# Attention and experts on one core: side work on eight of eighteen steps, a first list over two groups, and a cast of the queries that waits for the lower halves

## The chip, the cores and the metric

The kernel runs on one core of one Trainium2 chip. The metric is the device time of one execution in microseconds (us). The engines are named as in the profile: PE is TensorE (PEld its weight loads), DVE VectorE, ACT ScalarE, POOL GpSimd, SP SyncE, which issues most of the transfers. L12 is line 12 of the kernel before.

## What is computed

An attention whose queries are averaged in pairs, and behind it a mixture of experts with one expert for each token. The reference, cut:

```python
# q, k, v: (8, 8, 1152, 64): batch, heads, sequence, head width
q_pool = q.reshape(B, H, S // 2, 2, D).mean(axis=3)
scores = np.matmul(q_pool, k.transpose(0, 1, 3, 2)) / np.sqrt(D)
attn = np.exp(scores - np.max(scores, axis=-1, keepdims=True))
attn = attn / (np.sum(attn, axis=-1, keepdims=True) + 1e-09)
x = np.matmul(attn, v)               # then (batch, position, head * width): 4608 tokens of 512
# experts: w_gate (512, 8), modality_bias (2, 8), w1 (8, 512, 1024), w2 (8, 1024, 512)
logits = x @ w_gate + modality_bias[modality_id]
e_idx = np.argmax(logits, axis=1)
gate_w = softmax(logits)[token, e_idx]
out[token] = gate_w * (np.maximum(x[token] @ w1[e_idx], 0.0) @ w2[e_idx])
```

The outputs are float32. The kernel reaches this with 16-bit floats: a number is split into a high part and a rest ("hi" and "lo", "qh" and "lo", "VH" and "vl"), and the products of both parts are added up.

## The kernel before

**Attention (0 to about 735 us).** Two batches of one head make a *pair* of heads; there are 32 pairs and 18 *steps* for each, so a pair takes about 22 us. In one step TensorE makes the scores of a third of a row block (L906, L907, tile `psc`), ScalarE their exponentials (L908, tile `Pe`), and VectorE or ScalarE their *lower halves* (the low 16 bits of the exponential, L891 and L889, tile `Pl`); three steps later TensorE multiplies `Pe` and `Pl` with the values (L965 to L967, tile `xp`).

**The max pass.** The scores need the maximum of each query's row before their exponentials. It is found one pair ahead: the max pass of pair p begins 24 steps before the pair's own first step (T_MAX), one matmul of the rounded queries `QB` with the rounded keys `hi` a step (L839, tile `pm`), and a maximum on VectorE (L840). The result `mr` goes by a transfer (L820) into one row of `B`, the matrix that the scores read. There are two `QB`, for even and odd pairs.

**What is prepared for a pair.** The loads of keys and queries (L643, L644) are 46 steps ahead; GpSimd's sum of neighbouring queries (L658, `split_q`) is 34 steps ahead; its cast to 16 bits, `qh` (L667, `split_qh`), 26 steps ahead, and behind it two transfers (L628) put `qh` into `QB`. Then come the rests `lo` (L695, three operations on GpSimd, two of them issued 26 steps ahead), and the transfers of all of it into `B`. The value's high part `VH` is on GpSimd (L786), 14 and 15 steps ahead.

**Holds.** `hold(x, y)` makes the instruction x of GpSimd wait for the instruction y of VectorE, though it needs none of its data. `fast[0]` is the L891 that was issued last, and with `p > HELD` the sum of the queries, one operation of VH and one of lo are held on it, another lo on VectorE's `vl` of the pair before. The cast L667 isn't held.

**Scales.** Each pair's x is scaled by a power of two. `scales` (L753) makes five small operations on VectorE: `half`, two columns of `sc`, a column of `scales` and 64 rows of `both` (L757); one of them holds what another has.

**Side work.** The router's work goes on between the steps: one generator after another in the list `side`, which may make a piece at the end of a step. A group is eight pairs (1152 tokens, nine tiles of 128); there are four. At the end of each group's last pair `route(g)` is put into the list, and behind group 2 `first_list`, which counts the tokens of each expert in the first three groups (27 tiles), gives each token its place in a block (`place`, L459 to L505) and then makes lists of token numbers by small matmuls (`listing`, L507 to L556). It holds its listing until step 576 - 127 (T_LIST). What is left at the end of the attention is made before the experts start.

**The order.** The order of PE, ACT, DVE and POOL is the order of the program; SP's order is made by the framework's scheduler. POOL and SP wait in order: an instruction that waits holds up those behind it.

**Experts (about 735 to 1125 us).** Blocks of 256 tokens of one expert: tokens are gathered from `xs` in HBM by number, multiplied with w1 and w2, and scattered to the output. The first six blocks (NA) take their tokens from the first list. The first block's w1 comes in four loads (L1595) that are issued in the last pair, at steps 1 to 3 of it, into the buffers of the raw queries, keys and values; ScalarE splits them (L1599).

Of the kernel before, what the change touches and what calls it, by code (L numbers as in the profile page):

```python
# [9 lines left out]
F32 = mybir.dt.float32  # L10
# [12 lines left out]
P = 128  # L23
# [5 lines left out]
S = 1152  # L29
# [9 lines left out]
NSTEP = 2 * NKC  # L39
NR = 4  # L40
W3 = 3 * SQ
HELD = 3
BANK = W3 // 4
T_LIST = -127
PL = 2
RS = (4, 4, 2, 2)
SLOW_P = 1
# [71 lines left out]
SW = 3  # L119
PR = 2  # L120
NF = 4
T_W0 = (1, 3, 2, 3)
W1D = 0
T_W1 = (6, 4, 10, 11)
E1 = 1
# [40 lines left out]
class Router:  # L166
# [11 lines left out]
    def setup(self, ids, w_gate, bias):  # L178
        nc, con = self.nc, self.con
        wg = con.tile([P, 4, E], F32, name="wg")  # L180
        nc.sync.dma_start(out=wg, in_=w_gate.rearrange("(c p) e -> p c e", p=P))
        self.wg = con.tile([P, 4, 3, E], BF16, name="wg3")
        for i in range(3):
            nc.gpsimd.tensor_copy(self.wg[:, :, i], wg)
            if i < 2:
                nc.gpsimd.tensor_tensor(wg, wg, self.wg[:, :, i], op=ALU.subtract)
        self.b0 = con.tile([P, 2, E], F32, name="bias")
        nc.sync.dma_start(out=self.b0, in_=bias.rearrange("m e -> (m e)").unsqueeze(0).broadcast_to([P, 2 * E]).rearrange("p (m e) -> p m e", m=2))
        idt = con.tile([P, NTT, 2], I32, name="idt")
        nc.sync.dma_start(out=idt.rearrange("p t w -> p (t w)"), in_=ids.bitcast(I32))  # L190
        self.mid = con.tile([P, NTT], F32, name="mid")
        nc.gpsimd.tensor_copy(self.mid, idt[:, :, 0])
        self.up = con.tile([P, P], BF16, name="up")
        nc.gpsimd.memset(self.up, 1.0)
        nc.gpsimd.affine_select(out=self.up, in_=self.up, pattern=[[1, P]], compare_op=ALU.is_gt, fill=0.0, base=0, channel_multiplier=-1)
        self.id16 = con.tile([P, P], F16, name="id16")
        nc.gpsimd.tensor_copy(self.id16, self.ident)
        self.on = con.tile([P, P], BF16, name="on")
        nc.gpsimd.memset(self.on, 1.0)
        self.ie = self.iota("ie", E)  # L200
        self.ieE = self.iota("ieE", E, base=-E)
        self.lane16 = con.tile([P, P], BF16, name="lane16")
        nc.gpsimd.tensor_copy(self.lane16, self.iota("lane", P))
        self.part = self.iota("part", 1, cm=1)
        self.tile1 = self.iota("tile1", NTT, base=1)
        self.col = self.iota("col", 2 * (NBF - NA) + E)
        self.before = con.tile([P, E + 1, E], F32, name="before")
        nc.gpsimd.memset(self.before, 1.0)
        nc.gpsimd.affine_select(out=self.before, in_=self.before, pattern=[[1, E + 1], [-1, E]], compare_op=ALU.is_gt, fill=0.0, base=0,
                                channel_multiplier=0)  # L210
# [5 lines left out]
        self.added = {g: 0 for g in range(NTT // NT)}  # L216
        z = con.tile([P, NT, 2], F32, name="z")
        nc.gpsimd.memset(z, 0.0)
        nc.sync.dma_start(out=self.xs[T - NT * P:T, DM:XW].rearrange("(t p) d -> p t d", p=P), in_=z)
        self.pos = con.tile([P, NTT], F32, name="pos")  # L220
        self.exp = con.tile([P, NTT], F32, name="exp")

    def iota(self, name, n, base=0, cm=0):
        a = self.sm.tile([P, P], I32, name="io")[:, 0:n]
# [12 lines left out]
        self.nc.scalar.activation(w, self.wg[:, cc], AF.Copy, scale=isc)  # L237
        return w

    def token_scale(self, p, isc):  # L240
# [4 lines left out]
        isc(self.scales[g][:, h:h + 1])  # L245

    def turned(self, x, o):

# [127 lines left out]
    def first_blocks(self):  # L376
# [26 lines left out]
        c3 = sm.tile([P, NA, E], F32, name="own3A")  # L403
        nc.vector.tensor_tensor(c3, self.col[:, 0:NA].unsqueeze(2).broadcast_to([P, NA, E]), cut[:, 1:].unsqueeze(1).broadcast_to([P, NA, E]), op=ALU.is_ge)
        yield
        ef = sm.tile([P, NA], F32, name="ownA")
        nc.vector.tensor_reduce(ef, c3, op=ALU.add, axis=AX.X)
        yield
        self.ownA = self.con.tile([P, NA], I32, name="ownerA")
        nc.vector.tensor_single_scalar(self.ownA, ef, float(E - 1), op=ALU.min)  # L410

    def other_blocks(self):
        nc, sm = self.nc, self.sm
# [43 lines left out]
    def place(self, nt, late):  # L457
# [4 lines left out]
        wide = lambda i: sm.tile([P, nt, E], F32, name=f"ohp{nt}_{i}") if late else sm.tile([P, 3, NT, E], F32, name=f"wide{i}").rearrange("p q t e -> p (q t) e")  # L462
        oh = wide(0)
        nc.vector.tensor_tensor(oh, self.exp[:, 0:nt].unsqueeze(2).broadcast_to([P, nt, E]), be(self.ie), op=ALU.is_equal)
        yield
# [89 lines left out]
    def indices(self, n, acc, name):  # L555
# [10 lines left out]
        nc.vector.scalar_tensor_tensor(si, m, BIG, v, op0=ALU.mult, op1=ALU.add)  # L566
        return gi, si

    def first_list(self):

        for _ in self.first_blocks():
            yield 1
        for _ in self.place(3 * NT, False):
            yield PL
        yield T_LIST
        acc = self.con.tile([P, 2, 2 * NA], F32, name="accA")
        yield from self.listing(3, 2 * NA, acc)
        self.idxA = self.indices(2 * NA, acc, "A")

    def other_list(self):  # L580
# [7 lines left out]
def attention(tc, ctx, att, ident, npairs, xpool, on_two, on_split, on_scale, jobs, side, set_pm, started, ahead, hip):  # L588
# [36 lines left out]
        assert all((p, n) in made for n in names), f"pair {p}: {names} are not made yet"  # L625

    def move(o, i):
        nc.sync.dma_start(out=o, in_=i)  # L628

    half_q = lambda i: slice(i * 288, (i + 1) * 288)  # L630

# [30 lines left out]
    def split_qh(p):  # L662
        s = st[p]
        qh = s["qh"]
        made.add((p, "qh"))
        if p > 1:
            (nc.gpsimd if QH_POOL else nc.vector).tensor_copy(qh, s["q"][:, 0:SQ])  # L667
# [53 lines left out]
    def place_k(p, heads):  # L721

        s = st[p]
        for i in range(2):
            for j in heads:
                move(s["B1"][half[i], kcol(j)], s["hi"][half[j]])

    def place_lo(p, heads, k):

# [22 lines left out]
    def scales(p, pt):  # L752
        s = st[p]  # L753
        half = sm.tile([P, 1], I32, name="half", bufs=1)
        nc.vector.tensor_single_scalar(half, pt[:, 0:1].bitcast(I32), 24, op=ALU.logical_shift_right)
        sc = sm.tile([P, 2], I32, name="sc")
        power_of = lambda o, h, sign, e: nc.vector.tensor_scalar(o, h, sign * 2.0 ** 23, e * 2.0 ** 23, op0=ALU.mult, op1=ALU.add)  # L757
        power_of(sc[:, 0:1], half, -1, 205)
        power_of(sc[:, 1:2], half, 1, 49)
        s["sc"], s["isc"] = sc.bitcast(F32)[:, 0:1], sc.bitcast(F32)[:, 1:2]  # L760
        on_scale(p, lambda o: power_of(o, half, 1, 49))
        if p % 2 == 0:
            s["both"] = xpool.tile([P, 1], I32, name="both", bufs=3)
        r = slice(p % 2 * D, (p % 2 + 1) * D)
        power_of(st[p - p % 2]["both"][r], half[r], 1, 49)

    flat = lambda a: a.rearrange("p c j d -> p (c j) d")

# [149 lines left out]
    def split_x(p, x2):  # L918

        s = st[p]  # L920
        if p % 2 == 0:
            s["x"] = [xpool.tile([P, NT, 2 * D], F16, name=f"x{i}", bufs=1) for i in range(2)]
        hs = slice((p % 2) * D, (p % 2 + 1) * D)
        xh, xl = st[p - p % 2]["x"]
        nc.scalar.activation(xh[:, :, hs], x2[:, :, hs], AF.Copy, scale=s["sc"])
        if p % 2:
            s["xt"] = [xpool.tile([P, NT, P], F16, name=f"xt{i}", bufs=1) for i in range(2)]
            turn_part(p, 0, xh)
        later(XL, lambda: split_xl(p, x2))

    def split_xl(p, x2):
# [4 lines left out]
        if p % 2:  # L936
            turns.append(lambda: turned(p, xh, xl))
            if p + 2 >= npairs or (p + 2, "row9") in made:
                turns.pop(0)()

    def turned(p, xh, xl):
        s = st[p]
# [157 lines left out]
        busy(2)  # L1100
        advance(mxq, 1)
    busy(2)
    at(T_RT, 0, started)

    for p in range(npairs):
        b = NSTEP * p
# [27 lines left out]
    if ahead:  # L1134
        last = (npairs - 1) * NSTEP
        room = []

        def early():
            a, *r = [pa.tile([P, S], F32, name="raw" + x) for x in "qqkkv"]
            room.extend(r)  # L1140
            ahead[0](a)

        at(last + T_G0, 0, early)
        at(last + T_X0, 0, lambda: running.append(ahead[1](lambda: ps_max.tile([P, 512], F32, name="pm"))))
        for i in range(NF):
            at(last + T_W0[i], 0, lambda i=i: ahead[2](i, room[i]))
            at(last + T_W1[i], 0, lambda i=i: later_end(W1D, ahead[3](i)))
    running, wait = [], 0
    for t in range(NSTEP * npairs):
# [20 lines left out]
        if side and t >= wait:  # L1170
            r = next(side[0], DONE)
            if r is DONE:
                side.pop(0)
            else:
                wait = t + (r or 1) if (r or 1) > 0 else NSTEP * npairs + r
    for t in range(NSTEP * npairs, NSTEP * npairs + 40):
        now[0] = t
        advance(pvq, 9)
# [16 lines left out]
def gather_x(nc, rt, j, tile_):  # L1195

    x = []
    for h in parts(j):
        x.append(tile_(h))
        nc.gpsimd.indirect_dma_start(out=x[h][:, :], out_offset=None, in_=rt.xs[0:3 * NT * P if j < NA else T, :],  # L1200
                                     in_offset=bass.IndirectOffsetOnAxis(ap=index(rt, j, h)[0], axis=0))
    return x

# [345 lines left out]
def attention_moe(tc, att, ids, w_gate, bias, w1, w2, out):  # L1549
    nc = tc.nc  # L1550
    with ExitStack() as ctx:
# [9 lines left out]
        def on_two(n, x2):  # L1561
# [96 lines left out]
```

## Time and profile before

| | us |
|---|---|
| median of three runs | 1127.4 (1127.33 to 1129.1) |
| the profiled execution | 1126.72 |
| its span in the profile | 1125.0 |
| of this, TensorE busy | 1102.0 |
| VectorE busy | 972.0 |
| ScalarE busy | 913.3 |
| GpSimd busy | 414.2 |

All of the trace is from the profiled execution; its time has 1.7 us around the span. The clock that TensorE was granted is 1.00 in all stretches shown below. How to read the rows: in the timeline a row is the start and the duration in us, the engine, the line, the operation, the tiles out<-in and the shape, and in brackets how long the engine had been idle and what ended that. In a group by line, "x64 | 6.9, 149" is 64 instructions, 6.9 us busy, 149 ns for one. In the table by stretch a cell is an engine's busy time with its instructions.

### The profile page before, as it was taken

Reading aid. Unit: us, or ns where it says so; the run is one execution under the profiler, and the core shown is the slowest. Engines: PE = TensorE matmul, PEld = TensorE weight load, DVE = VectorE, ACT = ScalarE, POOL = GpSimd, SP = SyncE. Lnnn points to the kernel's source line nnn. Section 1 sums busy time; section 2 is a strip of 40 time slices with the busy share of each in tenths; the row PEclk is TensorE's granted clock in tenths of the full one; section 3 lists DMA queues with packets and bytes.
Section 4 is the critical chain, followed back from the end, with each engine's and each line's share of the span. In section 5 each row is a group of like instructions: output and inputs, shape, how many; then the busy total and the mean of one; then the engine's idle time right before and its main releaser. Section 6 shows DMA issues by size and latency. Waiting matters only on the chain.

```text
span 1125.0 us, 36836 instructions
## 1 busy us (share of the span) xinstructions
PE 1102.0 (98%) x15069; PEld 812.7 (72%) x15069; DVE 972.0 (86%) x1971; ACT 913.3 (81%) x1465; POOL 414.2 (37%) x408
## 2 busy tenths in 40 slices
PE   7999999999999999999999999999999999999997
PEld 3777777777777777777777777777667667667665
DVE  7999999999999999999999999877996766756755
ACT  5999999999999999999999998876556656655654
POOL 7753344355434444443445334115213112122111
PEclk9999999999999999999999999999999999999999
DMA  7777757768669578678687663499999999899993
GB/s 231 181 186 169 197 159 189 188 158 187 171 165 210 152 176 183 165 185 182 171 183 171 160 147 97 144 302 289 285 264 278 299 286 267 279 280 262 296 269 110
DMA packets 175522, 232.67 MB, mean 207 GB/s; under 512 B 92303, under 2 KB 126751, under 8 KB 175344
## 3 DMA queue, kind: packets, MB, share of 16 engines
q1 hardware_dynamic: 169254, 210.45, 71.4%
q0 software_dynamic: 6080, 19.78, 6.7%
q8 instruction: 120, 1.97, 0.8%
q14 instruction: 58, 0.48, 0.1%
q10 hardware_dynamic: 10, 0.00, 0.0%
HBM read 146.11 MB, written 18.99 MB: 147 GB/s over the span
## 4 chain that ended last, share of the span: by engine, by line
PE 80%; DVE 16%; DMA 2%; issue 1%; ACT 1%; SPq 0%; POOL 0%; POOLq 0%; DVEq 0%
PE psc L907 9%; PE psc L906 9%; PE pm L839 8%; DVE mp L840 8%; PE xp L965 6%; PE xp L967 6%; PE ph L1318 6%; PE ph L1316 6%; PE ph L1317 6%; PE xp L966 6%; PE po L1423 6%; PE po L1425 6%; PE po L1424 6%; DVE Pl L891 2%; DVE vl L782 1%; DVE mp L848 1%
## 5 line engine op out<-in xcount | busy, mean ns | idle before, releaser
L908 ACT ACTIVATE Pe<-psc 128x432 int32<-128x432 f32 x768 | 376.8, 526 | 40.6 <-PE psc L907 32.2
L840 DVE TENSOR_REDUCE mp<-pm 128x1 f32<-128x512 f32 x566 | 371.6, 684 | 16.8 <-PE pm L839 10.1
L965 PE MATMUL xp<-VH,Pe 128*128 128x65 f16 x2880 | 372.5, 193 | 0.0
L967 PE MATMUL xp<-VS,Pl 128*128 128x65 f16 x2880 | 371.9, 193 | 0.4 <-DVE Pl L891 0.4
L966 PE MATMUL xp<-vl,Pe 128*128 128x64 f16 x2880 | 370.6, 192 | 0.0
L966 PEld LDWEIGHTS <-Pe 128*128 128x128 f16 x2880 | 267.6, 98 | 87.6
L906 PE MATMUL psc<-B 128*128 128x432 f16 (+2 forms) x1152 | 304.1, 286 | 1.7 <-ACT Pe L908 1.5
L907 PE MATMUL psc<-B 65*128 65x432 f16 (+2 forms) x1152 | 304.7, 287 | 0.7 <-DMA B<-mr 0.5
L965 PEld LDWEIGHTS <-Pe 128*128 128x128 f16 x2880 | 272.0, 98 | 42.3 <-issue 4.7
L967 PEld LDWEIGHTS <-Pl 128*128 128x128 f16 x2880 | 266.5, 97 | 0.6 <-DVE Pl L891 0.6
L889 ACT ACTIVATE Pl<-Pe 128x1152 f16<-128x1152 uint16 (+1 forms) x190 | 219.2, 1154 | 6.0
L839 PE MATMUL pm<-hi,QB 128*128 128x512 f16 x566 | 213.8, 379 | 4.2 <-DVE mp L840 3.0
L1318 PE MATMUL ph<-xpart,w1l 128*128 128x256 f16 x544 | 148.3, 273 | 0.0
L1317 PE MATMUL ph<-xpart,w1h 128*128 128x256 f16 x544 | 148.3, 273 | 0.0
L1316 PE MATMUL ph<-xpart,w1h 128*128 128x256 f16 x544 | 148.3, 273 | 0.0
L786 POOL TENSOR_SCALAR VH<-rawv,sc 128x512 f16<-128x512 f32 (+1 forms) x60 | 103.6, 1736 | 76.2 <-PE pm L839 35.6
L907 PEld LDWEIGHTS <-B 65*128 65x128 f16 x1152 | 112.9, 98 | 25.2 <-issue 2.5
L906 PEld LDWEIGHTS <-B 128*128 128x128 f16 x1152 | 112.5, 98 | 7.9 <-issue 2.5
L1322 DVE SCALAR_TENSOR_TENSOR hl<-ph,hh 128x512 f16<-128x512 f32 x72 | 49.6, 689 | 76.6 <-ACT hh L1321 71.7
L1321 ACT ACTIVATE hh<-ph 128x512 f16<-128x512 f32 x72 | 43.0, 598 | 85.1 <-PE ph L1318 85.0
L1425 PE MATMUL po<-w2h,hl 128*128 128x512 f16 x288 | 109.2, 379 | 0.0
L1424 PE MATMUL po<-w2l,hh 128*128 128x512 f16 x288 | 109.2, 379 | 0.0
(288 smaller groups left out, 1881.3 us busy)
## 6 DMA issues: line engine op xcount, KB each, us to landing
w2r<-in_w_dram SPq DMA_DIRECT2D x76, 512.0 KB
w1r<-in_w_dram SPq DMA_DIRECT2D x72, 512.0 KB
rawv<-in_att_dram SPq DMA_DIRECT2D x32, 576.0 KB
B<-hi SPq DMA_DIRECT2D x128, 144.0 KB
rawq<-in_att_dram SPq DMA_DIRECT2D x31, 576.0 KB
rawk<-in_att_dram SPq DMA_DIRECT2D x31, 576.0 KB
B<-qh SPq DMA_DIRECT2D x128, 72.0 KB
B<-lo SPq DMA_DIRECT2D x64, 144.0 KB
```

What stands on the lines that cost most here:

```text
L839: nc.tensor.matmul(pm, QB[p % 2][:, u], s["hi"][:, t * 512:(t + 1) * 512], start=True, stop=True)
L840: nc.vector.tensor_reduce(mp[:, u, t:t + 1], pm, op=ALU.max, axis=AX.X)
L889: nc.scalar.activation(low, rest, AF.Copy, scale=LOW)
L906: nc.tensor.matmul(o, b1[:, ks], b1[:, qs], start=True, stop=False, skip_group_check=True)
L907: nc.tensor.matmul(o, b2[:, ks], b2[:, qs], start=False, stop=True, skip_group_check=True)
L908: nc.scalar.activation(Pe[:, D + x0:D + x1], pt, AF.Exp, scale=1.0 / 16)
L965: nc.tensor.matmul(out, Ph[:, qs], vh[:, c, j, 0:D + 1], start=c == 0 and g == 0, stop=False, skip_group_check=True)
L966: nc.tensor.matmul(out[:, 0:D], Ph[:, qs], vl[:, c, j], start=False, stop=False, skip_group_check=True)
L967: nc.tensor.matmul(out, Pl[:, qs], vs[:, c, j, 0:D + 1], start=False, stop=c == NKC - 1, skip_group_check=True)
L1316: nc.tensor.matmul(o, hi[:, c, fs], xh[:, :, c], start=c == 0, stop=False)
L1317: nc.tensor.matmul(o, hi[:, c, fs], xl[:, :, c], start=False, stop=False)
L1318: nc.tensor.matmul(o, lo[:, c, fs], xh[:, :, c], start=False, stop=c == 3)
```

## The change

1. `split_qh`: the cast of the queries on GpSimd is held on `fast[0]`, as the sum of them is.
2. HELD is 2 instead of 3, so that pair 3's operations are held too.
3. `scales`: two operations fewer on VectorE; GpSimd copies the column of `scales` to `both`.
4. The router's set-up is a generator of nine pieces in the list of side work, instead of one block at step 24.
5. Side work is made at the steps 1 to 4 and 13 to 16 of a pair alone (QUIET), and T_LIST is gone.
6. The first list is over two groups (GA): `first_place` stands behind the route of group 1, the listing behind that of group 2, and the blocks of the first list gather from two groups' rows of `xs`.
7. The four first loads of w1 are issued 12 steps before the last pair's first step, on SP behind the last pair's transfers of `hi`.
8. The first of the two DMA transposes of x goes, like the second, behind the transfer of `mr`.

The tokens of this input go to two experts in nearly equal parts; the blocks of the experts are the same before and after.

```diff
-HELD = 3
+HELD = 2
+ST = 4
-T_LIST = -127
+GA = 2
+QUIET = (1, 2, 3, 4, 13, 14, 15, 16)
-T_W0 = (1, 3, 2, 3)
+T_W0 = -12
+T_R0 = -13
...
     def setup(...):
...
+        yield
+        self.up = con.tile([P, P], BF16, name="up")
...
+        yield ST
...
+        yield ST
...
     def first_blocks(self):
...
-        ef = sm.tile([P, NA], F32, name="ownA")
-        nc.vector.tensor_reduce(ef, c3, op=ALU.add, axis=AX.X)
-        yield
-        self.ownA = self.con.tile([P, NA], I32, name="ownerA")
-        nc.vector.tensor_single_scalar(self.ownA, ef, float(E - 1), op=ALU.min)
+        self.efA = self.con.tile([P, NA], F32, name="ownA")
+        nc.vector.tensor_reduce(self.efA, c3, op=ALU.add, axis=AX.X)
...
+    def first_place(self):
+
+        for _ in self.first_blocks():
+            yield PL
+        for _ in self.place(GA * NT, False):
+            yield PL
+
     def first_list(self):
 
-        for _ in self.first_blocks():
-            yield 1
-        for _ in self.place(3 * NT, False):
-            yield PL
-        yield T_LIST
+        self.ownA = self.con.tile([P, NA], I32, name="ownerA")
+        self.nc.vector.tensor_single_scalar(self.ownA, self.efA, float(E - 1), op=ALU.min)
+        yield 1
         acc = self.con.tile([P, 2, 2 * NA], F32, name="accA")
-        yield from self.listing(3, 2 * NA, acc)
+        yield from self.listing(GA, 2 * NA, acc)
         self.idxA = self.indices(2 * NA, acc, "A")
...
         if p > 1:
-            (nc.gpsimd if QH_POOL else nc.vector).tensor_copy(qh, s["q"][:, 0:SQ])
+            done = (nc.gpsimd if QH_POOL else nc.vector).tensor_copy(qh, s["q"][:, 0:SQ])
+            if p > HELD:
+                hold(done, fast[0])
...
-                move(s["B1"][half[i], kcol(j)], s["hi"][half[j]])
+                s["placed"] = move(s["B1"][half[i], kcol(j)], s["hi"][half[j]])
...
-        sc = sm.tile([P, 2], I32, name="sc")
+        sc, isc = sm.tile([P, 1], I32, name="sc"), on_scale(p)
         power_of = lambda o, h, sign, e: nc.vector.tensor_scalar(o, h, sign * 2.0 ** 23, e * 2.0 ** 23, op0=ALU.mult, op1=ALU.add)
-        power_of(sc[:, 0:1], half, -1, 205)
-        power_of(sc[:, 1:2], half, 1, 49)
-        s["sc"], s["isc"] = sc.bitcast(F32)[:, 0:1], sc.bitcast(F32)[:, 1:2]
-        on_scale(p, lambda o: power_of(o, half, 1, 49))
+        power_of(sc, half, -1, 205)
+        power_of(isc, half, 1, 49)
+        s["sc"], s["isc"] = sc.bitcast(F32), isc.bitcast(F32)
...
-        power_of(st[p - p % 2]["both"][r], half[r], 1, 49)
+        nc.gpsimd.tensor_copy(st[p - p % 2]["both"][r], isc[r])
...
-            turn_part(p, 0, xh)
+            turns.append(lambda: turn_part(p, 0, xh))
...
+        def load_first(i):
+            with tc.issue_after(st[npairs - 1]["placed"].ins):
+                ahead[2](i, room[i + 1])
+
+        at(last + T_R0, 0, lambda: room.extend(pa.tile([P, S], F32, name="raw" + x) for x in "qqkkv"))
...
-            at(last + T_W0[i], 0, lambda i=i: ahead[2](i, room[i]))
+            at(last + T_W0, 0, lambda i=i: load_first(i))
...
-                wait = t + (r or 1) if (r or 1) > 0 else NSTEP * npairs + r
+                wait = t + (r or 1)
+                while wait % NSTEP not in QUIET:
+                    wait += 1
...
                 side.append(rt.route(g, eng))
+                if g == GA - 1:
+                    side.append(rt.first_place())
                 if g == 2:
                     side.append(rt.first_list())
```

GpSimd's order around a pair in the middle of the attention, before (the rows from one pair's sum of queries to the next one's; a row's "waits" are the queues and engines that it waits for):

```order
L658 TENSOR_TENSOR rawq<-rawq 128x576 [waits DMAHW3_49,DVE_49]
L786 TENSOR_SCALAR VH_125<-rawv,sc 128x8x64 [waits DMAHW4_49,DVE_49,PE_49]
L786 TENSOR_SCALAR VH_125<-rawv,sc 128x10x64
L667 CAST qh<-rawq 128x576 [waits DMAHW2_49,DMAHW3_49,DMAHW1_49,DMAHW7_49,DMAHW0_49,Pool_49]
L695 TENSOR_TENSOR lo<-rawq,qh 128x576 [waits DMAHW6_49,DMAHW5_49,DMAHW7_49,DVE_49,Pool_49]
L695 TENSOR_TENSOR lo<-rawk,hi 128x576 [waits DMAHW0_49,DVE_49]
L695 TENSOR_TENSOR lo<-rawk,hi 128x576 [waits Activation_49]
L658 TENSOR_TENSOR rawq<-rawq 128x576 [waits DMAHW0_49,DVE_49]
```

The same place on GpSimd after the change (L672 is the sum, L801 VH, L681 the cast, L711 the rests, L780 the new copy):

```order
L780 COPY both<-scales 64x1 [waits DVE_49]
L672 TENSOR_TENSOR rawq<-rawq 128x576 [waits DMAHW1_49]
L801 TENSOR_SCALAR VH_125<-rawv,sc 128x8x64 [waits DMAHW7_49,DVE_49,PE_49]
L801 TENSOR_SCALAR VH_125<-rawv,sc 128x10x64
L681 CAST qh<-rawq 128x576 [waits DMAHW5_49,DMAHW0_49,DMAHW6_49,DVE_49,Pool_49]
L711 TENSOR_TENSOR lo<-rawq,qh 128x576 [waits DMAHW2_49,DMAHW1_49,DMAHW3_49,DMAHW0_49,Pool_49]
L711 TENSOR_TENSOR lo<-rawk,hi 128x576 [waits DMAHW4_49,Activation_49]
L711 TENSOR_TENSOR lo<-rawk,hi 128x576 [waits Activation_49]
```

The cast now waits for VectorE (DVE_49), and the two rests behind it no longer do so themselves; the copy to `both` is ahead of the next sum and waits for VectorE in its place.

SyncE's order from one pair's load of the values to the transfer of its rests, before (QB are the rounded queries of the max pass, mr the row of maxima):

```order
L648 DMA rawv<-in_att_dram 128x1152
L628 DMA QB_112<-qh 64x576 x2
L232 DMA xs<-x_7533 128x9x128
L628 DMA B_0_111<-qh 64x576
L643 DMA rawq<-in_att_dram 128x1152
L949 DMA_TRANSPOSE xt_8529<-x_7979 128x9x128
L820 DMA B_1_113<-mr 1x9x128
L949 DMA_TRANSPOSE xt_8530<-x_7980 128x9x128
L628 DMA B_0_111<-lo 64x1152
```

The same stretch of SyncE after the change:

```order
L662 DMA rawv<-in_att_dram 128x1152
L244 DMA xs<-x_4131 128x9x128
L642 DMA QB_112<-qh 64x576 x2
L642 DMA B_0_111<-qh 64x576
L657 DMA rawq<-in_att_dram 128x1152
L835 DMA B_1_113<-mr 1x9x128
L965 DMA_TRANSPOSE xt_5126<-x_4577 128x9x128
L965 DMA_TRANSPOSE xt_5127<-x_4578 128x9x128
L642 DMA B_0_111<-lo 64x1152
```

The store of x (`xs`) is now ahead of the transfers to QB, and both transposes are behind the transfer of mr.

More of the change, by code (lines that the diff above doesn't have):

```diff
@@ L190, in setup @@
         nc.sync.dma_start(out=idt.rearrange("p t w -> p (t w)"), in_=ids.bitcast(I32))
[L191 to L210, printed above, removed]
         self.base = self.keep.tile([P, E], F32, name="base")
@@ L216, in setup @@
         self.added = {g: 0 for g in range(NTT // NT)}
+        self.pos = con.tile([P, NTT], F32, name="pos")
+        self.exp = con.tile([P, NTT], F32, name="exp")
+        yield
+        self.up = con.tile([P, P], BF16, name="up")
+        nc.gpsimd.memset(self.up, 1.0)
+        nc.gpsimd.affine_select(out=self.up, in_=self.up, pattern=[[1, P]], compare_op=ALU.is_gt, fill=0.0, base=0, channel_multiplier=-1)
+        yield ST
+        self.id16 = con.tile([P, P], F16, name="id16")
+        nc.gpsimd.tensor_copy(self.id16, self.ident)
+        self.on = con.tile([P, P], BF16, name="on")
+        nc.gpsimd.memset(self.on, 1.0)
+        yield ST
+        self.ie = self.iota("ie", E)
+        self.mid = con.tile([P, NTT], F32, name="mid")
+        nc.gpsimd.tensor_copy(self.mid, idt[:, :, 0])
+        yield ST
+        self.ieE = self.iota("ieE", E, base=-E)
+        self.part = self.iota("part", 1, cm=1)
+        yield ST
+        self.lane16 = con.tile([P, P], BF16, name="lane16")
+        nc.gpsimd.tensor_copy(self.lane16, self.iota("lane", P))
+        yield ST
+        self.tile1 = self.iota("tile1", NTT, base=1)
+        self.col = self.iota("col", 2 * (NBF - NA) + E)
+        yield ST
+        self.before = con.tile([P, E + 1, E], F32, name="before")
+        nc.gpsimd.memset(self.before, 1.0)
+        nc.gpsimd.affine_select(out=self.before, in_=self.before, pattern=[[1, E + 1], [-1, E]], compare_op=ALU.is_gt, fill=0.0, base=0,
+                                channel_multiplier=0)
+        yield ST
         z = con.tile([P, NT, 2], F32, name="z")
@@ L219, in setup @@
         nc.sync.dma_start(out=self.xs[T - NT * P:T, DM:XW].rearrange("(t p) d -> p t d", p=P), in_=z)
-        self.pos = con.tile([P, NTT], F32, name="pos")
-        self.exp = con.tile([P, NTT], F32, name="exp")
+        yield ST
     def iota(self, name, n, base=0, cm=0):
@@ L238, in gate_weights, with token_scale @@
         return w
-    def token_scale(self, p, isc):
+    def token_scale(self, p):
         g, h = divmod(p, H)
@@ L244, in token_scale @@
             self.scales[g] = self.keep.tile([P, H], I32, name="scales")
-        isc(self.scales[g][:, h:h + 1])
+        return self.scales[g][:, h:h + 1]
     def turned(self, x, o):
@@ L461, in place @@
         yield
-        wide = lambda i: sm.tile([P, nt, E], F32, name=f"ohp{nt}_{i}") if late else sm.tile([P, 3, NT, E], F32, name=f"wide{i}").rearrange("p q t e -> p (q t) e")
+        wide = lambda i: sm.tile([P, nt, E], F32, name=f"ohp{nt}_{i}") if late else sm.tile([P, 3, NT, E], F32, name=f"wide{i}").rearrange("p q t e -> p (q t) e")[:, 0:nt]
         oh = wide(0)
@@ L627, in move @@
     def move(o, i):
-        nc.sync.dma_start(out=o, in_=i)
+        return nc.sync.dma_start(out=o, in_=i)
     half_q = lambda i: slice(i * 288, (i + 1) * 288)
@@ L938, in split_xl @@
             if p + 2 >= npairs or (p + 2, "row9") in made:
-                turns.pop(0)()
+                while turns:
+                    turns.pop(0)()
     def turned(p, xh, xl):
@@ L1102, in attention, with start_side @@
     busy(2)
-    at(T_RT, 0, started)
+    def start_side():
+        setting = started()
+        next(setting)
+        side.insert(0, setting)
+    at(T_RT, 0, start_side)
     for p in range(npairs):
@@ L1136, in attention @@
         room = []
[L1138 to L1143, printed above, removed]
+        def load_first(i):
+            with tc.issue_after(st[npairs - 1]["placed"].ins):
+                ahead[2](i, room[i + 1])
+        at(last + T_R0, 0, lambda: room.extend(pa.tile([P, S], F32, name="raw" + x) for x in "qqkkv"))
+        at(last + T_G0, 0, lambda: ahead[0](room.pop(0)))
         at(last + T_X0, 0, lambda: running.append(ahead[1](lambda: ps_max.tile([P, 512], F32, name="pm"))))
         for i in range(NF):
-            at(last + T_W0[i], 0, lambda i=i: ahead[2](i, room[i]))
+            at(last + T_W0, 0, lambda i=i: load_first(i))
             at(last + T_W1[i], 0, lambda i=i: later_end(W1D, ahead[3](i)))
@@ L1199, in gather_x @@
         x.append(tile_(h))
-        nc.gpsimd.indirect_dma_start(out=x[h][:, :], out_offset=None, in_=rt.xs[0:3 * NT * P if j < NA else T, :],
+        nc.gpsimd.indirect_dma_start(out=x[h][:, :], out_offset=None, in_=rt.xs[0:GA * NT * P if j < NA else T, :],
                                      in_offset=bass.IndirectOffsetOnAxis(ap=index(rt, j, h)[0], axis=0))
```

## The prediction

> **What bounds the kernel now.** I read the page first, for the bound over the whole span, then a table of TensorE's busy time by stretch, then the timeline around the one edge that the change adds.
>
> ```profile
> span 1125.0 us, 36836 instructions
> PE 1102.0 (98%) x15069; PEld 812.7 (72%) x15069; DVE 972.0 (86%) x1971; ACT 913.3 (81%) x1465; POOL 414.2 (37%) x408
> ```
>
> TensorE is busy for 1102.0 of 1125.0 us, so a part of the change can win only where TensorE idles, and loses wherever it makes TensorE wait. The table by stretch (us, TensorE's busy time, instructions, granted clock, DMA share, GB/s) says where it idles:
>
> ```profile
> 24.00:68.00 44.00, 40.98 (x660) 1.00 0.67 177
> 24.00:200.00 176.00, 171.60 (x2908) 1.00 0.70 175
> 200.00:560.00 360.00, 359.78 (x6243) 1.00 0.74 177
> 700.00:740.00 40.00, 38.33 (x727) 1.00 0.59 186
> 200.00:400.00 200.00, 199.83 (x3462) 154.57 (x3460) 192.01 (x428) 190.38 (x326) 87.52 (x73) 1.00 0.75 178
> 740.00:1100.00 360.00, 360.00 (x2557) 244.94 (x2556) 259.06 (x380) 220.30 (x284) 78.77 (x78) 1.00 0.99 279
> ```
>
> The last two rows have all engines, in the order TensorE, its weight loads, VectorE, ScalarE, GpSimd. TensorE idles 4.40 us in the first eight pairs (176.00 - 171.60), 3.02 of it before 68; 0.22 in all of 200 to 560, and 1.67 in the change to the experts (700 to 740). The experts have none: no part of the change acts there, since the blocks and their matmuls stay. In the steady pairs VectorE is busy 192.01 of 200 so it has 0.88 us to spare in a pair of 22 us, and TensorE has nothing.
>
> For the list region a second measure is better, since a short pause between matmuls hides under their modelled ends: the first matmul of each max pass is a mark that returns once a pair.
>
> ```profile
> 40.02 0.38 PE L839 MATMUL pm<-hi,QB 128*128 128x512 f16 x1
> 174.19 0.38 PE L839 MATMUL pm<-hi,QB 128*128 128x512 f16 x1
> 306.06 0.38 PE L839 MATMUL pm<-hi,QB 128*128 128x512 f16 x1
> 328.24 0.38 PE L839 MATMUL pm<-hi,QB 128*128 128x512 f16 x1
> 349.83 0.38 PE L839 MATMUL pm<-hi,QB 128*128 128x512 f16 x1
> 569.82 0.38 PE L839 MATMUL pm<-hi,QB 128*128 128x512 f16 x1
> 685.94 0.38 PE L839 MATMUL pm<-hi,QB 128*128 128x512 f16 x1
> ```
>
> These are passes 2, 8, 14, 15, 16, 26 and 31. A steady pair takes 22.18 from an even pass to the odd one, 21.59 back. Passes 26 to 31 take 116.12, steady ones would take 3 x 22.18 + 2 x 21.59 = 109.72: the list region costs **6.4 us**. Passes 8 to 26 take 395.63 against 9 x 43.77 = 393.93, so 1.7.
>
> **The edge that the change adds.** GpSimd's cast of the queries (L667) now also waits for VectorE's last lower halves (L891). Pair 14 (even), in order of time, and the four rows of pair 15 (odd) behind the "...":
>
> ```profile
> 299.31 0.66 POOL L667 CAST qh<-rawq 128x576 f16<-128x576 f32 x1
> 299.59 0.70 DVE L891 TENSOR_SCALAR Pl<-Pe 128x576 f16<-128x576 uint16 x1
> 300.00 1.10 SPq L628 DMA_DIRECT2D QB<-qh  x2
> 301.19 0.54 SPq L232 DMA_DIRECT2D xs<-x  x1
> 302.19 1.29 POOL L695 TENSOR_TENSOR lo<-rawq,qh 128x576 f16<-128x576 f32 x1 [2.21 <-issue]
> 303.77 0.44 DVE L891 TENSOR_SCALAR Pl<-Pe 128x576 f16<-128x576 uint16 x1
> 304.29 1.28 POOL L695 TENSOR_TENSOR lo<-rawk,hi 128x576 f16<-128x576 f32 x1 [0.82 <-DVE Pl L891]
> 306.11 0.45 DVE L891 TENSOR_SCALAR Pl<-Pe 128x576 f16<-128x576 uint16 x1
> ...
> 320.94 0.66 POOL L667 CAST qh<-rawq 128x576 f16<-128x576 f32 x1
> 323.81 1.28 POOL L695 TENSOR_TENSOR lo<-rawq,qh 128x576 f16<-128x576 f32 x1 [2.22 <-DMA rawv<-in_att_dram]
> 324.79 0.62 DVE L891 TENSOR_SCALAR Pl<-Pe 128x576 f16<-128x576 uint16 x1
> 325.49 1.28 POOL L695 TENSOR_TENSOR lo<-rawk,hi 128x576 f16<-128x576 f32 x1 [0.40 <-DVE Pl L891]
> ```
>
> Which L891 it will be can be read now: `lo<-rawk,hi` is issued in the same step as the cast and held on the same instruction, and its row shows that it was released at 304.29 by the L891 that ended at 304.21. The cast then starts at about 304.29, not 299.31: **4.98 us later**, and behind it stand both QB transfers, which the first matmul of the max pass at 306.06 reads. What must follow: a release of 0.08 (304.29 - 304.21), the cast 0.66, the issue of the first of two transfers 1.10 / 2 = 0.55, and its landing. The trace has no row for a QB landing. The nearest is a small transfer that TensorE was seen to wait for:
>
> ```profile
> 15.64 1.46 ACTq L820 DMA_DIRECT2D B<-mr  x1
> 18.59 0.34 PE L907 MATMUL psc<-B 65*128 65x432 f16 x1 [0.53 <-DMA B<-mr]
> B<-qh SPq DMA_DIRECT2D x128, 72.0 KB
> ```
>
> It was issued until 17.10 and landed at 18.59: 1.49. A QB transfer carries as much as one `B<-qh`, 72.0 KB; at the 177 GB/s of 200 to 560 that is 0.41 more if it had to share all of that traffic. I take 1.49, because rawv, which was issued ahead of QB, has had five more microseconds to drain, and keep 0.41 for the range. The need is 0.08 + 0.66 + 0.55 + 1.49 = 2.78.
>
> Even pairs: the L891 at 299.59 took 0.70 beside the cast and 0.44 without (303.77), so with the cast gone VectorE runs 0.26 ahead; L891 ends at 303.95, QB is there at 306.73, and TensorE stands from 306.06: **0.67 us**. Odd pairs: L891 took 0.62 beside `lo` and ended at 325.41; with 0.44 it ends at 325.23, and QB is there at 328.01, before 328.24: nothing, with 0.23 to spare. The even pairs from 4 to 26 are twelve: 12 x 0.67 = **8.0 us lost**. The pairs behind 26 are longer (116.12 / 5 = 23.2), and I take nothing there. The ends: nothing at all (rival A), and 0.41 more in every pair (rival B); a gain from a later cast has no row for it.
>
> **The other parts.**
>
> (a) GpSimd's early load: pair 3's operations are held as well, the router's set-up comes in nine pieces over four pairs instead of one block in pair 1, and two scale operations leave VectorE:
>
> ```profile
> L757 DVE TENSOR_SCALAR sc<-half 128x1 int32<-128x1 int32 x64 | 6.9, 149 | 1.1
> L757 DVE TENSOR_SCALAR both<-half 64x1 int32<-64x1 int32 x32 | 4.6, 143 | 0.2
> L327 POOL COPY gt<-ts 128x9 f32<-128x9 f32 x4 | 0.8, 192 | 6.7 <-DVE ts L324 6.7
> ```
>
> That is 0.149 + 0.143 = 0.29 us of VectorE in each pair, for one GpSimd copy of about 0.19 (the nearest row). GpSimd is 37% busy, so the copy is hidden; the 0.29 pays only where TensorE waits for VectorE. Of the 4.40 us idle before 200 I take half, 2.2, bounds 0 and 4.4: the start of pair 1 also fills its pipes, which no edit touches.
>
> (b) The list: its place part (VectorE's small operations over 27 tiles, from the first row below on) leaves the region for pairs 22 to 26, now over 18 tiles; two groups remain of three.
>
> ```profile
> 633.85 0.38 DVE L464 TENSOR_TENSOR wide<-exp,ie 128x216 f32<-128x216 f32 x1
> L515 DVE TENSOR_TENSOR ol<-lof,lane 128x384 bf16<-128x384 bf16 x21 | 12.1, 581 | 0.0
> L526 DVE TENSOR_TENSOR r<-o,tile 128x342 bf16<-128x342 f32 (+1 forms) x7 | 3.2, 460 | 0.0
> L547 PE MATMUL pm<-r,ol 128*128 128x24 bf16 x27 | 1.0, 174 | 0.0
> ```
>
> A group costs 3 x 0.581 and three others of at most 0.46 each, some 3 us of VectorE, and nine matmuls, 1.0 / 3 = 0.3. Of the 6.4 us of the region I take 3.5: the last group, its rows and the fourth route stay. Bounds 0 and 6.4. The moved pieces land where VectorE has 0.88 us a pair; at 0.38 for the largest and two or three in a pair they fit, so I take nothing; the ends are 1.7 to the good (what passes 8 to 26 lose now) and as much to the bad.
>
> (c) Side work only at eight of eighteen steps moves pieces by a few steps; its gain is in (a) and (b). (d) The first weights are issued before the last pair's maximum row. In the trace ScalarE, and behind it TensorE, waited for them:
>
> ```profile
> 718.83 1.06 ACT L1599 ACTIVATE w1h<-rawk 128x1024 f16<-128x1024 f32 x1 [0.91 <-DMA rawk<-in_w_dram]
> ```
>
> I take 0.7 of this 0.91, bounds 0 and 1.67 (all idle of 700 to 740). (e) Both transposes now go behind the row's transfer: SyncE's queue holds QB, rawq, row, transpose, transpose. Nothing in 200 to 560 waits for the row, so nothing. The store of x, now ahead of QB there, was issued at 301.19 and is out before QB's new time. Behind the held cast GpSimd has the two `lo`: the first, at 302.19 now, ends at about 306.0 instead of 303.48, and the reload of rawq that needs its end, and is ahead of the row on SyncE, is 2.5 later; the row has until the next pair's scores.
>
> **The sum.** Gains 2.2 + 3.5 + 0.7 = 6.4, loss 8.0: 1126.7 (the profiled execution) + 1.6 = 1128.3. The runs' median, 1127.4, is 0.7 above the profiled one; with half of that I say **1128.7**. A difference of 0.2%, 2.3 us, is about what a measurement of this kernel can tell from no change.
>
> **The rivals.** *A: the hold costs nothing*, since QB lands in time, or TensorE's stand is made up. Then only the gains are left: 1126.7 - 6.4 = 1120.3. For it: nothing in the trace waits for QB today, and the landing is borrowed from another transfer. Against: it must take 0.67 less than 2.78. Also here: the parts of (a) and (b) that do what they say beyond my halves.
>
> *B, slower: QB lands later than the small row did.* By 0.41 even pairs lose 1.08 and odd ones 0.18: 12 x 1.08 + 11 x 0.18 = 14.9, less 6.4, gives 1126.7 + 8.5 = 1135.2. It decides between the landing of 1.49 and 1.90: from 0.23 on the odd passes stand as well. For it: the DMA engines are busy 0.74 of the time. Against: rawv is out of the way by then.
>
> *C: the conflict moves instead of going.* The L891 at 324.79 began inside `lo` (323.81 to 325.09) and ended at 325.41, 0.32 behind it; that at 299.59 ended at 300.29, 0.32 behind the cast (299.97). So VectorE waits until GpSimd's operation is over, and the longest L891 is as long as a whole `lo` and itself:
>
> ```profile
> L891 DVE TENSOR_SCALAR Pl<-Pe x194: 442/451/1560, 23.3 to 733.7; 128x576 f16<-128x576 uint16 x182, 128x864 f16<-128x864 uint16 x12
> ```
>
> After the change the cast and two `lo` of 1.28 run back to back from about 304.0 to 307.3, and the L891 of 306.11 falls into the second: it would end 0.32 behind it, at 307.6 instead of 306.56, 1.0 later. The 0.88 to spare, with 0.29 from the scales and 0.26 from the cast, covers that if it lies at the right place; if a third of it reaches TensorE in each of 23 pairs, that is 7.7, and 1128.3 + 7.7 = 1136.
>
> The Trainium skill, in "SBUF — State Buffer" under "Who interferes with whom", says that the pair of ports that VectorE and GpSimd share is an exclusive lock held for a whole instruction, and that whoever comes first blocks the other. The two equal ends of 0.32 agree with it. By this rule the hold takes VectorE's wait from one operation of 0.66 to one of 1.28, and C is what it makes of the time where nothing covers it.
>
> **How the numbers follow.** My forecast 0.43, within 1124 to 1132; A 0.30; B 0.14; C 0.13. Faster by over 0.2% (below 1125.1): A but for 0.01, and 0.05 of the forecast: 0.34. Slower (above 1129.7): B, most of C (0.11), and 0.15 of the forecast: 0.40. Within: 0.26. The range 1119 to 1136.5 leaves out what lies beyond A's gains and the worse half of B and C.
>
> **What would show it.** The cast's row right behind an L891 and 5 us later than now; in even passes a row of the first L839 with some 0.7 us idle before it, released by a DMA of QB, in odd ones none; 200 to 560 with about 8 us idle instead of 0.22; L891 at 0.45 beside no cast; less idle in 24 to 68 and 640 to 680; L1599 without its wait. I am wrong if L839 never waits for QB, or waits in odd pairs too, or if L840 or L967 wait for a late L891.

## The result, and the profile after

The changed kernel takes 1143.16 us (median of 5 runs, 1142.39 to 1147.16) against 1127.33 (5 runs): ratio 1.0141, 95% interval 1.013 to 1.0153. It is 16 us slower, where 1128.7 with a range of 1119 to 1136.5 was predicted. The profiled execution, 1147.16, is the slowest of the five, at a mean granted clock of 0.992 where the median one has 0.998; its size is used below with care, its places freely.

The page and the table by stretch of the changed kernel (us, TensorE's busy time, instructions, granted clock, DMA share, GB/s):

```profile
span 1145.1 us, 36752 instructions
PE 1108.3 (97%) x15060; PEld 814.1 (71%) x15060; DVE 989.8 (86%) x1900; ACT 919.3 (80%) x1465; POOL 434.8 (38%) x440
...
L854 PE MATMUL pm<-hi,QB 128*128 128x512 f16 x566 | 215.0, 381 | 21.4 <-DMA QB<-qh 18.3
L906 DVE TENSOR_SCALAR Pl<-Pe 128x576 f16<-128x576 uint16 (+1 forms) x194 | 121.8, 628 | 4.1 <-ACT Pe L923 3.1
```

```profile
24.00:200.00 176.00, 169.44 (x2840) 0.99 0.67 170
200.00:560.00 360.00, 345.39 (x5935) 1.00 0.69 170
700.00:740.00 40.00, 39.66 (x707) 1.00 0.61 143
```

The same two groups of instructions in the kernel before:

```profile
L839 PE MATMUL pm<-hi,QB 128*128 128x512 f16 x566 | 213.8, 379 | 4.2 <-DVE mp L840 3.0
L891 DVE TENSOR_SCALAR Pl<-Pe 128x576 f16<-128x576 uint16 (+1 forms) x194 | 100.2, 517 | 3.5 <-ACT Pe L908 2.3
```

The stretch that had been full, 200 to 560, now has 14.61 us of idle instead of 0.22. The two groups name the causes: TensorE's max pass (L854, L839 before) waits 18.3 us for the transfer of QB, a wait that did not exist before, and the lower halves (L906, L891 before) take 628 ns on average instead of 517, 21.6 us more of VectorE. A list of what TensorE waited for (us in total, times, the longest) gives the count:

```profile
PE pm L854 <- DMA QB<-qh: 18.3, 21, 2.3
```

21 waits, the longest of 2.3 us, are far more than the twelve of 0.67 that were forecast. The timeline of the same two pairs (14, and behind the "..." 15) shows both effects:

```profile
311.22 0.45 DVE L906 TENSOR_SCALAR Pl<-Pe 128x576 f16<-128x576 uint16 x1
311.80 0.67 POOL L681 CAST qh<-rawq 128x576 f16<-128x576 f32 x1 [5.30 <-issue]
312.49 1.49 SPq L642 DMA_DIRECT2D QB<-qh  x2
312.55 1.28 POOL L711 TENSOR_TENSOR lo<-rawq,qh 128x576 f16<-128x576 f32 x1
312.60 1.84 DVE L950 SCALAR_TENSOR_TENSOR x<-x,sc,x 128x576 f16<-128x576 f32 x1
313.79 3.25 POOL L711 TENSOR_TENSOR lo<-rawk,hi 128x576 f16<-128x576 f32 x2
314.37 1.53 DVE L906 TENSOR_SCALAR Pl<-Pe 128x576 f16<-128x576 uint16 x1
314.86 0.39 PE L854 MATMUL pm<-hi,QB 128*128 128x512 f16 x1 [1.28 <-DMA QB<-qh]
...
334.87 2.00 SPq L642 DMA_DIRECT2D QB<-qh  x2
337.68 0.39 PE L854 MATMUL pm<-hi,QB 128*128 128x512 f16 x1 [0.33 <-DMA QB<-qh]
```

Here the cast stands behind its L906, and the chain L906, cast, QB, L854 is the one that was foretold. Two things in it were not. In pair 14 QB's first transfer was issued by about 313.0 and read at 314.86, 1.9 later instead of 1.49; and in pair 15, odd, TensorE waits as well, which the prediction had named as a sign of being wrong. Between them VectorE loses time to the two rests: L950 takes 1.84 where it takes 0.81 alone (and 1.05 in pair 14 before), and L906 1.53 instead of 0.45.

### The profile page after: what moved, and what is told of

Same layout as the page of the kernel before. It is cut to its first block, busy times and chain, and to the rows that moved or that the text cites. A ratio compares the mean times of both kernels' runs of the same rounds, so it can differ in the third digit from the quotient of the medians.

```text
span 1145.1 us, 36752 instructions
## 1 busy us (share of the span) xinstructions
PE 1108.3 (97%) x15060; PEld 814.1 (71%) x15060; DVE 989.8 (86%) x1900; ACT 919.3 (80%) x1465; POOL 434.8 (38%) x440
## 4 chain that ended last, share of the span: by engine, by line
PE 62%; DVE 19%; issue 9%; DMA 6%; POOL 2%; ACT 1%; POOLq 0%; DVEq 0%; ACTq 0%
DVE mp L855 10%; PE pm L854 6%; PE ph L1339 5%; PE ph L1341 5%; PE ph L1340 5%; PE psc L922 5%; PE po L1446 5%; PE po L1447 5%; PE po L1448 5%; PE psc L921 5%; DMA QB<-qh 5%; PE xp L981 4%; PE xp L983 3%; PE xp L982 3%; DVE Pl L906 3%
## 5 line engine op out<-in xcount | busy, mean ns | idle before, releaser
L923 ACT ACTIVATE Pe<-psc 128x432 int32<-128x432 f32 x768 | 382.1, 527 | 55.3 <-PE psc L922 46.7
L854 PE MATMUL pm<-hi,QB 128*128 128x512 f16 x566 | 215.0, 381 | 21.4 <-DMA QB<-qh 18.3
L906 DVE TENSOR_SCALAR Pl<-Pe 128x576 f16<-128x576 uint16 (+1 forms) x194 | 121.8, 628 | 4.1 <-ACT Pe L923 3.1
L801 POOL TENSOR_SCALAR VH<-rawv,sc 128x512 f16<-128x512 f32 (+1 forms) x60 | 103.5, 1734 | 22.9 <-PE pm L854 11.4
L1446 PE MATMUL po<-w2h,hh 128*128 128x512 f16 x288 | 109.2, 379 | 0.0
```

The lines of the kernel that those rows point to most:

```text
L854: nc.tensor.matmul(pm, QB[p % 2][:, u], s["hi"][:, t * 512:(t + 1) * 512], start=True, stop=True)
L923: nc.scalar.activation(Pe[:, D + x0:D + x1], pt, AF.Exp, scale=1.0 / 16)
```

## The experiments

All times are medians; a ratio is against the kernel before, run beside it. "Marks" are the first matmuls of max passes 8 and 26: 395.63 us lie between them before, 414.42 after.

**The changed kernel without the hold on the cast.**

```diff
-            done = (nc.gpsimd if QH_POOL else nc.vector).tensor_copy(qh, s["q"][:, 0:SQ])
-            if p > HELD:
-                hold(done, fast[0])
+            (nc.gpsimd if QH_POOL else nc.vector).tensor_copy(qh, s["q"][:, 0:SQ])
```

> The changed kernel without the hold on the cast of the queries; all else as changed. If the hold is the whole loss: the 21 waits for QB (18.3 us) and the L906 of 1.53 are gone, and the time is that of the gains alone, about 1120 (1118 to 1123). If the side work at eight steps or the moved list costs as well: above 1127, with idle of TensorE between 200 and 560 that no QB row ends.

1121.04 us, ratio 0.9945 (0.9928 to 0.9962). No wait for QB; 200 to 560 is full again (second row), and the idle of the first pairs, of the list region (560 to 700, 3.79 before) and of the change to the experts is smaller than before:

```profile
24.00:200.00 176.00, 173.28 (x2945) 1.00 0.73 178
200.00:560.00 360.00, 359.50 (x6238) 1.00 0.74 177
560.00:700.00 140.00, 139.49 (x2414) 1.00 0.68 162
700.00:740.00 40.00, 39.08 (x672) 1.00 0.77 185
```

So the hold is the whole loss, 0.0196 of the ratio or **22 us**, and the other parts win 7.0 (1128.07 - 1121.04). This kernel beats both.

**The hold alone, in the kernel before.**

```diff
-            (nc.gpsimd if QH_POOL else nc.vector).tensor_copy(qh, s["q"][:, 0:SQ])
+            done = (nc.gpsimd if QH_POOL else nc.vector).tensor_copy(qh, s["q"][:, 0:SQ])
+            if p > HELD:
+                hold(done, fast[0])
```

> The kernel before with the hold on the cast and nothing else. If the hold is the whole loss and acts alone: as far above 1127 as the changed kernel stands above the one without the hold, 1148 to 1151. If it costs only together with the other parts (store of x ahead of QB, copy on GpSimd): under 1140.

1170.73, ratio 1.0377 (1.0356 to 1.0398): 43 us, twice the loss, which neither expectation had. The waits for QB rise to 29.6 us, the longest 2.9. SyncE's rows and TensorE's in one of the pairs with transposes:

```profile
323.64 1.32 SPq L951 DMA_TRANSPOSE xt<-x  x1
325.05 1.82 SPq L628 DMA_DIRECT2D QB<-qh  x2
328.40 0.39 PE L841 MATMUL pm<-hi,QB 128*128 128x512 f16 x1 [2.15 <-DMA QB<-qh]
```

With the cast late, the scheduler put a DMA transpose right ahead of QB on SyncE. Behind it TensorE stood for 2.15 us, and then its clock halved, as the table around this wait shows (the number behind the count is the granted clock):

```profile
326.00:328.00 2.00, 0.26 (x3) 1.00 0.72 155
328.00:330.00 2.00, 1.60 (x34) 0.96 0.73 144
330.00:331.00 1.00, 1.00 (x9) 0.50 0.94 357
331.00:333.00 2.00, 2.00 (x19) 0.50 1.09 178
```

**The hold and the transposes behind the row's transfer, in the kernel before.** The edit above, and part 8 of the change:

```diff
-            turn_part(p, 0, xh)
+            turns.append(lambda: turn_part(p, 0, xh))
...
-                turns.pop(0)()
+                while turns:
+                    turns.pop(0)()
```

> The kernel before with the hold and with both transposes behind the transfer of mr. With the hold alone the order of SyncE has a DMA transpose right ahead of QB in every other pair, and 42.7 us are lost, against 22 with all the other parts. If the transpose ahead of QB is the difference: 1146 to 1154, and the longest wait for QB falls from 2.9 to under 2. If the store of x ahead of QB or the scales make it: still over 1162.

1148.33, ratio 1.0175 (1.0154 to 1.0196). The longest wait for QB is 1.5 and the sum 15.5. So the transpose ahead of QB, with what the halved clock added to it, was 22 us of the 43.

**The second lo three steps later.** In the changed kernel, hold kept:

```diff
-T_LO = (-23, -26, -17, -19, -26, -17, -23)
+T_LO = (-23, -26, -17, -19, -23, -17, -23)
```

> The changed kernel, hold kept, but the second lo is issued three steps later (at step -23 and not -26), so that it is held on the next lower halves and can't stand in their way. Theory QB late (the chain from the hold to QB is too long, whatever VectorE does): L906 is back at 0.45, the waits for QB stay, 14 us or more, and the time stays over 1138. Theory blocked VectorE (the 1.1 us that L906 and some 1.0 that L950 lose beside lo make the next L906 late, and QB with it): the waits for QB fall under 9 us in the even pairs alone and the time to 1126 to 1131.

1138.65, ratio 1.0089 (1.0069 to 1.0109): 4.5 us less than the changed kernel, and 6.2 less between the marks (408.20). L906 is back:

```profile
L906 DVE TENSOR_SCALAR Pl<-Pe 128x576 f16<-128x576 uint16 (+1 forms) x194 | 94.0, 485 | 5.4 <-ACT Pe L923 4.4
PE pm L854 <- DMA QB<-qh: 15.0, 20, 1.3
```

The waits for QB fall only from 18.3 to 15.0. The signs that were named for a late QB came (L906 back, waits over 14, the time over 1138), and the fall to 1126 to 1131 that was named for a blocked VectorE did not. Still, 4.5 us went with the second lo, so the blocked VectorE takes part; where it does, the section on why the prediction was wrong takes up.

**Both lo together, without the hold on the cast.** In the changed kernel the hold on the cast goes, and the first lo is held on the same L906 as the second, so that the rests run one behind the other while QB is early:

```diff
+            vl_first.pop(p - 1, None)
-            hold(done, fast[0] if i else vl_first.pop(p - 1))
+            hold(done, fast[0])
```

> The changed kernel without the hold on the cast, but with the first lo held on the same lower halves as the second, so that both lo run one behind the other as in the changed kernel, while QB is early. Theory QB late: no wait for QB, the time within 1.5 us of the kernel without the hold (about 1120). Theory blocked VectorE: L906 is 0.7 to 1.5 once a pair and TensorE waits for VectorE (L855 or L906); 3 us or more above the kernel without the hold.

1128.36, ratio 1.0001 (0.9991 to 1.0011): 7.3 above the kernel without the hold, with no wait for QB. L905 (its line here) is 116.7 us in all against 98.6, and TensorE waits for VectorE's maxima instead, 4.8 us where it is 1.8 without any hold on the cast:

```profile
PE pm L853 <- DVE mp L854: 4.8, 15, 0.5
```

So the conflict with the rests costs TensorE by itself, where no wait for QB covers it.

**The cast two steps earlier, hold kept.**

```diff
-T_QH = -26
+T_QH = -28
```

> The changed kernel, hold kept, but the cast is issued two steps earlier (-28 and not -26), where the last lower halves issued are those of one L906 earlier (the one that runs about four us before). The cast then starts some 1 us later than without a hold, not 5. If the loss is the lateness of QB and the two lo in a row: no wait for QB, L906 at 0.45 beside the cast, time as without the hold or a little better, 1118 to 1121. If a hold on the cast costs in itself, wherever it ends: over 1126.

1123.27, ratio 0.9964 (0.995 to 0.9977). The same hold, on the L906 before, is 2.2 us slower than none by the medians; the intervals overlap, so neither a cost nor a gain is shown. The waits for QB are 0.8 us in two places. What costs is which L906 the hold names.

**The fetches shifted.** In the trace of the kernel with the second lo later, TensorE had QB 1.5 us after the end of its issue in pairs 4 to 7 and in 20, 22, 24 and 26, but 1.75 to 2.4 after it in the even ones of 8 to 18. Pair 18, and behind the "..." pair 20:

```profile
402.11 1.96 SPq L642 DMA_DIRECT2D QB<-qh  x2
404.81 0.39 PE L854 MATMUL pm<-hi,QB 128*128 128x512 f16 x1 [1.26 <-DMA QB<-qh]
...
448.56 1.11 SPq L642 DMA_DIRECT2D QB<-qh  x2
450.57 0.39 PE L854 MATMUL pm<-hi,QB 128*128 128x512 f16 x1 [0.58 <-DMA QB<-qh]
```

The two transfers take 0.85 longer to issue in pair 18. What stands beside them is in the DMA view of 402 to 405 (packets, MB, share of the engines):

```profile
q8 instruction: 1, 0.02, 2.2%
```

One packet of 16 KB of instructions. By the packets' times it began 0.06 us behind the end of QB's first issue in pair 18, and 1.07 behind it in pair 20. There is one for about 130 of TensorE's matmuls with their weight loads, so I take them for TensorE's; between 170 and 600 each takes 0.9 to 1.6 us. The edit adds 43 matmuls at the start, so that each fetch comes a third of that interval earlier:

```diff
+    busy(43, 64)
     busy(2)
```

> The kernel with the second lo later, with 43 more small matmuls on TensorE in its first 40 us (a third of the 131 matmuls between two fetches of its instructions), which shifts where the fetches of 16 KB fall. If the fetch beside QB is what makes QB land 1.8 to 3.2 us after its issue in pairs 8 to 19 rather than 1.5: the late landings move to other pairs (those of 8 to 18, even, back to about 1.5; some of 20 to 26 late), the time within 6 us of 1138.7. If the store of x or the loads ahead of QB do it: the same pairs stay late.

1133.88, ratio 1.0051 (1.0033 to 1.0069), 4.8 us less than with the second lo later alone, although work was added. Pair 18 again:

```profile
402.30 0.39 PE L854 MATMUL pm<-hi,QB 128*128 128x512 f16 x1 [0.53 <-DMA QB<-qh]
```

The even pairs 10, 12, 14, 18 and 20 to 26 now have QB 1.49 to 1.62 after its issue, 8 and 16 have 1.83 and 1.96, and the odd ones 9 to 25 don't wait any more. The late landings left the pairs that the fetch left. That they would turn up in 20 to 26 was wrong: there the fetch now lay 1.0 us or more ahead of QB. Pair 27, where it lay 0.04 ahead, did get later (2.09 instead of 1.70). Over the three kernels (as changed, second lo later, fetches shifted) and the pairs that waited, a landing was late where the fetch began within 0.8 us of the end of QB's issue, and about 1.5 where it was over 1 us away, with three exceptions: pair 7 as changed, and pairs 8 and 16 here.

**The transpose in its old place, without the hold.** The first kernel above, with part 8 taken back:

```diff
-            turns.append(lambda: turn_part(p, 0, xh))
+            turn_part(p, 0, xh)
...
-                while turns:
-                    turns.pop(0)()
+                turns.pop(0)()
```

> The kernel without the hold, with the first transpose ahead of the transfer of mr again, as before. If the place of the transpose matters only for a late QB: within 1.5 us of 1121.0, the kernel without the hold. If it is where the gain came from: 1124 or more.

1126.51, ratio 0.9988 (0.9976 to 1.0): some 5 us above the kernel without the hold (5.5 by the medians, 4.9 by the ratios), so the place of the transpose does matter. In the last pair a transpose takes 4.1 us to issue, behind the early loads of w1, and the row of maxima behind it is late:

```profile
700.58 4.10 SPq L962 DMA_TRANSPOSE xt<-x  x1
704.78 0.84 SPq L833 DMA_DIRECT2D B<-mr  x1
711.09 0.34 PE L920 MATMUL psc<-B 65*128 65x432 f16 x1 [2.77 <-DMA B<-mr]
```

Behind this pause TensorE's granted clock is 0.50 from 711.88 to 715.30. From mark 31 (685.94 before) to the first matmul of the experts this kernel takes 52.68 us, against 48.27 without the hold.

**And with the first weights as late as before.** On top of the last edit:

```diff
-T_W0 = -12
+T_W0 = (1, 3, 2, 3)
...
-            with tc.issue_after(st[npairs - 1]["placed"].ins):
-                ahead[2](i, room[i + 1])
+            ahead[2](i, room[i])
...
```

> As the run with the first transpose in its old place and without the hold (1126.5), but the first four loads of w1 are issued as late as before too. There TensorE waited 2.8 us for the row of the last pair, behind a transpose that took 4.1 us to issue behind the loads of w1. If the early loads make that wait: no wait of over 1 us for B<-mr, 1121 to 1125, and the wait of L1599's kind for w1 of about 0.9 us is back. If the transpose's place costs by itself: still 1126 or more.

1122.6, ratio 0.9947 (0.9932 to 0.9963). The wait of 2.77 is gone, so the early loads had made it: parts 7 and 8 belong together, and both taken back cost nothing that these runs tell from the kernel without the hold. From mark 31 to the experts it takes 48.22 us. The wait of ScalarE for w1 came back at 0.17 us, not the 0.91 expected.

## Why the prediction was wrong

**The gains were right.** 6.4 was the sum, 7.0 the measurement (the interval of the ratio gives 4 to 8). By place: the first pairs 4.40 - 2.72 = 1.7 us of idle for 2.2; passes 26 to 31 take 111.74 without the hold instead of 116.12, so 4.4 for 3.5; idle of 700 to 740 0.8 for 0.7. The first two terms were picks inside wide bounds, and no run takes parts 2 to 6 apart, so their nearness is in part luck and which part made them stays open. The reason of the third failed: the early weights were credited with 0.7 and the moved transposes with nothing. Without the moved transposes the early loads lose some 5 us, and with both undone the stretch from mark 31 to the experts is as short as with both (48.22 and 48.27, 49.20 before). That 0.7 came out was luck.

**The loss was found and mis-sized: 8.0 was the term, 22 the measurement.** The edge, the L906 it names, the delay of the cast and the chain behind it were as told. The steps that failed are "I take 1.49", a landing of QB that was held constant, and the "nothing" for the odd passes that hung on it. The landing does have 1.49 as its least value, but it ran up to 3.2. Between marks 8 and 26 the 19.1 us that the hold adds (414.42 - 395.32 without it) come apart by the runs:

- **Late QB with the fetches away from it: 8.9** (404.17 with the second lo later and the fetches shifted). The nine even passes that lie there were forecast at 0.67 each, 6.0; in that run each begins 0.91 later behind the pass before than without the hold, 8.2 in all, and the odd ones add 0.7. This step held, somewhat small. The first lo still blocks L950 there (1.74 to 1.84 in the even pairs); what that costs is in the 8.9, and no run separates it.
- **"I take 1.49": 4.0** (408.20 - 404.17). The landing isn't a constant. In pairs 8 to 19 a fetch of TensorE's instructions beside QB adds 0.3 to 1.7 us, and with it the odd passes stand too, since they had 0.23 to spare. This is rival B, at 0.14; its size was about right and its reason (full traffic) wrong: in the two us ahead of the end of QB's first issue the DMA engines are busy for 0.12 of the time at most in passes 8 to 26 of the changed kernel. That the fetch keeps QB's rows waiting on the DMA engine that serves it is the likeliest reading, but was only argued; that the late landings go with the fetch is shown, with the three exceptions above.
- **"Covers that": 6.2** (414.42 - 408.20), **and not by the way that rival C priced.** What C foretold came: L906 ends 0.32 behind the second lo, at 1.53 us, and in the even pairs L950, which reads two tiles in SBUF, is blocked by the first lo as well. But from mark 8 to mark 20 it made 0.5 us of difference (274.15 against 273.61 with L906 back at 0.45), since TensorE stands for QB there in any case. The other 5.7 lie in passes 21 to 26. In 21 and 24 the cast came 0.5 later behind the mark of the pass before than with the second lo later, and so QB met a fetch (it began 0.69 and 0.78 behind the end of QB's first issue instead of 1.14 and 1.12): it landed 3.20 and 2.93 after its issue, and the two passes cost 3.7 more. In pass 24 TensorE stood for 2.31 us, its clock was halved from 546.79 to 550.21, and pass 25 cost 1.6 more. The median execution, at a mean clock of 0.998, has hardly had such a stretch, so the difference of the medians, 4.5, is the better size. Why the cast was later in these passes and not in most others stays open.

Ahead of mark 8 the "nothing" for the odd passes failed without any fetch: passes 5 and 7 stood for 0.34 and 0.41 us with QB 1.49 and 1.56 after its issue, so the 0.23 that was read off pair 15 wasn't there in the first pairs.

So B and C were treated as alternatives of 0.14 and 0.13, with the middle of the forecast at neither. Both came about, and they act on one chain: in most passes the wait for QB hides VectorE's delay, and in a few the delay puts QB beside a fetch and makes the wait longer. The Trainium skill, "SBUF — State Buffer", "Who interferes with whom", lists a VectorE operation with two SBUF inputs among those that contend with a GpSimd operation that reads SBUF, beside the exclusive lock that the prediction drew on: the 1.84 of L950 beside lo agrees, and this sentence of it was not applied to L950.

**That the order on SyncE can decide** was missed in "(e) ... so nothing": that argument held for the kernel before, where nothing waited for QB. With the hold alone the scheduler's order has a transpose ahead of QB, and moving it is worth 22 us; with the early weights and no hold it is worth some 5.

## What to carry to other kernels

A wait that is added "for the port" is a wait on the whole chain behind the waiting instruction: before adding one, measure from the end of the instruction it names to the first reader of the last transfer behind it, and leave a microsecond or more for landings that vary. A hold moves a conflict to what runs next; count every operation on the other engine that meets the released row of work, not one of them. Where two rivals act on the same chain, work both out at once instead of choosing: one can hide in the wait that the other makes, or make that wait longer.

## What the runs showed of the hardware

- **A pause of about 2 us can halve TensorE's clock for 3.4 us.** In the hold-alone kernel the records of the granted clock have nine stretches at 0.50 between 20 and 745 us, seven of 3.4 us and two of 6.8, each 1.7 to 3.8 us behind the start of a pause of 1.65 to 2.9 us between two matmuls; in the kernel before, with no pause over 1.21, there is none. It isn't a sharp limit: six pauses of 1.43 to 1.56 in four of the kernels and one of 1.92 were not followed by a stretch, and one of 1.22 was (the kernel with the hold and the moved transposes, at 630 us). A stretch of 3.4 us at 0.50 costs up to 1.7 us on top of the wait. The Trainium skill, "TensorE: Matmul & The Clock Gate", "Why this matters for your kernels", gives about 3 us as the longest pause to allow; here 2.15 us of idle was too long.
- **The instruction stream shares the DMA engines with the data.** A fetch of 16 KB for TensorE takes 0.9 to 1.6 us about every 7.6 us (the kernel with the second lo later, 170 to 600), and a transfer of 72 KB issued beside it lands up to 1.7 us later. Adding 43 small matmuls far ahead in the program made a kernel 4.8 us faster.
- **A blocked lower half ends 0.3 us behind the operation that blocks it, whichever that is**: 0.32 behind the cast, which takes 0.66, and 0.32 behind a rest, which takes 1.28 or, where it was itself held up, 1.79.
